# Attention with pooled keys, then a residual MLP, on one core: the second program moved to GpSimd alone, and the last store moved to ScalarE's queue

## The chip, the cores and the metric

One core of one Trainium2 chip runs the kernel. The time is device microseconds of one execution: the median of three runs is 333.9 us (333.8 to 334.21). A core has five engines with an instruction stream each: TensorE (PE; its weight loads are shown apart as PEld), VectorE (DVE), ScalarE (ACT), GpSimd (POOL) and SyncE (SP, which here only issues DMAs). SP, ACT and POOL each have a queue of DMAs of their own. All queues feed the same 16 DMA engines, and so does the loading of the engines' instructions.

## What is computed

Shapes: `q`, `k`, `v` are (8 batches, 8 heads, 576 tokens, 64), all float32.

```python
k_p = k.reshape(B, H, 72, 8, D).mean(axis=3)          # 8 neighbours pooled
v_p = v.reshape(B, H, 72, 8, D).mean(axis=3)
scores = (1 / sqrt(D)) * q @ k_p.T                     # (B, H, 576, 72)
attn = exp(scores - max(scores)) / (sum(exp(scores - max(scores))) + 1e-9)
x = (attn @ v_p), heads side by side                   # (B, 576, 512)
u = x + lam * (w_tok @ (alpha1 * x + beta1))           # mixing of tokens
out = u + lam * (relu((alpha2 * u + beta2) @ w_ch1) @ w_ch2)   # 512 -> 2048 -> 512
```

## The kernel before

There are two programs in one kernel. `direct` (L202) computes the result in 16-bit matmuls and takes exp without subtracting the maximum. That holds only while the sums of the exponentials stay within bounds, so `direct` also checks its sums: near its end, `all_in_range` (L249) and `count_in_range` (L261) reduce the saved reciprocals of all sums to one number, `fine`, which is 1 where all lie in range. The last function (L1226) then loads `fine` into a register (L1234), on PE, ACT and POOL, and enters `tc.If(good < 1)` (L1235): the second program, `general` (L24), computes everything again, safely and slowly, over the same output. With the inputs given here `fine` is 1. `general` is never entered: its instructions lie in memory behind those of `direct`, and the engines that take part in it branch past them.

`general` before uses PE (transposes and matmuls), ACT (copies out of PSUM, exp, relu) and POOL (elementwise work and all DMAs). Hence the three engines at L1234: each loads `fine`, compares, and either runs its part or jumps behind it. Behind it, the end of the program is common to all five engines (shown at L1262): SP waits for every semaphore in turn, those of the DMA queues among them, so for the landing of every store; then all engines meet in two barriers, between which POOL clears the semaphores.

`direct` works in blocks of 512 rows of tokens, nine in all (`NBLK`). Each block goes through `mlp_A` (L851: 512 -> 2048, relu on ACT) and then the second matrix. From block 2 on that second product is Winograd's form of Strassen's scheme: `hidden_sum` and `weight_sum` on DVE, seven `product`s (L958, matmuls at L985), and `gather` (L989, the additions into `u_sb` on DVE at L1000 and L1003). The order of instructions in each block is written out by hand: `todo` is a list of (due time, action), sorted at L1221, and no scheduler moves anything afterwards.

In the last block the stores are cut in halves of 256 columns (L1186 to L1193). `store` (L893) issues one DMA on `queues[0]` for a chunk of 128 rows (L898), and two of 64 rows, on `queues[0]` and `queues[1]`, for a chunk shared by two batches (L902). The last actions of all are the gather of product 3 (two DVE additions at L1000, rows `m` = 0 and 1, columns 256 to 511) and, due at 29.2, the two stores of just these rows. Before, both go on SP's queue:

```python
todo.append((27.2, lambda m=m: store(n, 2 + m, 0, HALF, (nc.sync, nc.scalar))))
todo.append((29.2, lambda m=m: store(n, m, HALF, DM)))     # queues=(nc.sync, nc.sync)
```

ACT's own last DMA is the second 64-row half of the store due at 27.2 (L902). Behind it in ACT's stream stand the load of `fine` and the branch. In PE's stream these stand behind the last matmul of L985, in POOL's behind its last multiplication for the attention of batch 7 (L771).

Of the kernel before, what the change touches and what calls it, by code (L numbers as in the profile page):

```python
# [7 lines left out]
FP = mybir.dt.float32  # L8
# [6 lines left out]
P = 128  # L15
# [8 lines left out]
def general(  # L24
# [18 lines left out]
    B, H, S, D = q.shape  # L43
    sb = ctx.enter_context(tc.tile_pool(name="g_sb", bufs=1))
    tmp = ctx.enter_context(tc.tile_pool(name="g_tmp", bufs=2))
    ps_s = ctx.enter_context(tc.tile_pool(name="g_ps", bufs=2, space=bass.MemoryType.PSUM))
    ps_l = ctx.enter_context(tc.tile_pool(name="g_psl", bufs=2, space=bass.MemoryType.PSUM))

    def tok(c):
        return (P if c < 4 else REM), slice(P * c, min(P * c + P, S))  # L50

    ident = sb.tile([P, P], FP, tag="ident", name="g_ident")
    nc.gpsimd.memset(ident, 0.0)
    nc.gpsimd.affine_select(out=ident, in_=ident, compare_op=ALU.not_equal, fill=1.0, base=0,
                            pattern=[[-1, P]], channel_multiplier=1)
    pool = sb.tile([P, 16], FP, tag="pool", name="g_pool")
    nc.gpsimd.memset(pool, 0.125)
    nc.gpsimd.affine_select(out=pool, in_=pool, compare_op=ALU.is_ge, fill=0.0, base=0,
                            pattern=[[-8, 16]], channel_multiplier=1)
    nc.gpsimd.affine_select(out=pool, in_=pool, compare_op=ALU.is_ge, fill=0.0, base=7,  # L60
                            pattern=[[8, 16]], channel_multiplier=-1)
    pools = sb.tile([P, 5, SPG], FP, tag="pools", name="g_pools")
    nc.gpsimd.memset(pools, 0.0)
    for c in range(5):
        n = 16 if c < 4 else 8
        nc.gpsimd.tensor_copy(out=pools[:, c, 16 * c:16 * c + n], in_=pool[:, 0:n])

    minus = sb.tile([P, 1], FP, tag="minus", name="g_minus")
    nc.gpsimd.memset(minus, -1.0)

    def smaller(out, a, b):


        d = tmp.tile([P, SPG], FP, tag="d", name="g_d")[0:a.shape[0], 0:a.shape[1]]
        nc.gpsimd.tensor_tensor(out=d, in0=a, in1=b, op=ALU.subtract)
        nc.scalar.activation(out=d, in_=d, func=AF.Relu, bias=0.0, scale=1.0)
        nc.gpsimd.tensor_tensor(out=out, in0=a, in1=d, op=ALU.subtract)

    vec = {}
    for name, src in (("a1", alpha1), ("b1", beta1), ("a2", alpha2), ("b2", beta2), ("lam", lam)):  # L80
        vec[name] = sb.tile([P, DM], FP, tag=f"vec_{name}", name=f"g_{name}")
        nc.gpsimd.dma_start(out=vec[name], in_=src.unsqueeze(0).to_broadcast((P, DM)))
    w1 = sb.tile([P, 4, DFF], FP, tag="w1", name="g_w1")
    nc.gpsimd.dma_start(out=w1, in_=w_ch1.rearrange("(c p) j -> p c j", p=P))
    w2 = sb.tile([P, NJ, DM], FP, tag="w2", name="g_w2")
    nc.gpsimd.dma_start(out=w2, in_=w_ch2.rearrange("(j p) d -> p j d", p=P))

    def transposed(src, rows, cols):
        ps = ps_s.tile([P, P], FP, tag="t", name="g_pt")
        nc.tensor.transpose(out=ps[0:cols, 0:rows], in_=src, identity=ident[0:rows, 0:rows])  # L90
        return ps[0:cols, 0:rows]

    wT = sb.tile([P, 5, S], FP, tag="wT", name="g_wT")
    for c in range(5):
        n, rows = tok(c)
        w = sb.tile([P, S], FP, tag="w_tok", name="g_w")
        nc.gpsimd.dma_start(out=w[0:n], in_=w_tok[rows])
        for i in range(5):
            m, cols = tok(i)
            nc.scalar.copy(out=wT[0:m, i, rows], in_=transposed(w[0:n, cols], n, m))  # L100

    for b in range(B):
        raw = []
        for src in (q, k, v):
            t = sb.tile([P, 5, H, D], FP, tag=f"raw{len(raw)}", name="g_raw")
            for c in range(5):
                n, rows = tok(c)
                nc.gpsimd.dma_start(out=t[0:n, c], in_=src[b, :, rows].rearrange("h p d -> p h d"))
            raw.append(t)
        means = []  # L110
        for t in raw[1:]:
            ps = ps_l.tile([P, DM], FP, tag="l", name="g_pl")
            for c in range(5):
                n, _ = tok(c)
                nc.tensor.matmul(out=ps[0:SPG], lhsT=pools[0:n, c],
                                 rhs=t[0:n, c].rearrange("p h d -> p (h d)"),
                                 start=(c == 0), stop=(c == 4))
            m = sb.tile([SPG, H, D + 1], FP, tag=f"mean{len(means)}", name="g_mean")
            nc.gpsimd.memset(m, 1.0)
            nc.scalar.copy(out=m[:, :, 0:D], in_=ps[0:SPG].rearrange("p (h d) -> p h d", d=D))  # L120
            means.append(m)
        kp, vp = means
        x = sb.tile([P, 5, DM], FP, tag="x", name="g_x")
        for h in range(H):
            cols = slice(D * h, D * h + D)
            kT = tmp.tile([D, SPG], FP, tag="kT", name="g_kT")
            nc.scalar.copy(out=kT, in_=transposed(kp[:, h, 0:D], SPG, D))
            for c in range(5):
                n, _ = tok(c)
                qT = tmp.tile([D, P], FP, tag="qT", name="g_qT")  # L130
                nc.scalar.copy(out=qT[:, 0:n], in_=transposed(raw[0][0:n, c, h], n, D))
                sc = ps_s.tile([P, P], FP, tag="s", name="g_sc")[0:n, 0:SPG]
                nc.tensor.matmul(out=sc, lhsT=qT[:, 0:n], rhs=kT)
                neg = tmp.tile([P, SPG], FP, tag="neg", name="g_neg")
                nc.scalar.activation(out=neg[0:n], in_=sc, func=AF.Copy, bias=0.0, scale=-0.125)
                low = tmp.tile([P, SPG], FP, tag="low", name="g_low")
                src, size = neg, SPG
                while size > 1:
                    half = size // 2
                    smaller(low[0:n, 0:half], src[0:n, 0:half], src[0:n, half:2 * half])  # L140
                    if size % 2:
                        smaller(low[0:n, 0:1], low[0:n, 0:1], src[0:n, size - 1:size])
                    src, size = low, half
                E = tmp.tile([P, SPG], FP, tag="E", name="g_E")
                nc.scalar.activation(out=E[0:n], in_=neg[0:n], func=AF.Exp, bias=low[0:n, 0:1],
                                     scale=-1.0)
                ET = tmp.tile([SPG, P], FP, tag="ET", name="g_ET")
                nc.scalar.copy(out=ET[:, 0:n], in_=transposed(E[0:n], n, SPG))
                av = ps_s.tile([P, P], FP, tag="s", name="g_av")[0:n, 0:D + 1]
                nc.tensor.matmul(out=av, lhsT=ET[:, 0:n], rhs=vp[:, h])  # L150
                xv = tmp.tile([P, D + 1], FP, tag="xv", name="g_xv")
                nc.scalar.copy(out=xv[0:n], in_=av)
                nc.gpsimd.tensor_tensor(out=xv[0:n, D:D + 1], in0=xv[0:n, D:D + 1],
                                        in1=minus[0:n], op=ALU.pow)
                nc.gpsimd.tensor_tensor(out=x[0:n, c, cols], in0=xv[0:n, 0:D],
                                        in1=xv[0:n, D:D + 1].to_broadcast((n, D)), op=ALU.mult)
        a = sb.tile([P, 5, DM], FP, tag="a", name="g_a")
        for c in range(5):
            n, _ = tok(c)
            nc.gpsimd.tensor_tensor(out=a[0:n, c], in0=x[0:n, c], in1=vec["a1"][0:n], op=ALU.mult)  # L160
            nc.gpsimd.tensor_tensor(out=a[0:n, c], in0=a[0:n, c], in1=vec["b1"][0:n], op=ALU.add)
        aT = sb.tile([P, 4, S], FP, tag="aT", name="g_aT")
        for c in range(5):
            n, rows = tok(c)
            ps = ps_l.tile([P, DM], FP, tag="l", name="g_pl")
            for i in range(5):
                m, _ = tok(i)
                nc.tensor.matmul(out=ps[0:n], lhsT=wT[0:m, i, rows], rhs=a[0:m, i],
                                 start=(i == 0), stop=(i == 4))
            y = tmp.tile([P, DM], FP, tag="y", name="g_y")  # L170
            nc.scalar.copy(out=y[0:n], in_=ps[0:n])
# [4 lines left out]
            for cc in range(4):  # L176
                nc.scalar.copy(out=aT[:, cc, rows],
                               in_=transposed(y[0:n, P * cc:P * cc + P], n, P))
# [1088 lines left out]
```

## Time and profile before

| what | value |
|---|---|
| median of three runs | 333.9 us |
| the profiled execution, its own time | 334.24 us |
| its span, first to last instruction | 332.5 us |
| PE busy | 325.2 us (98%), 2531 matmuls |
| DVE, ACT, POOL busy | 236.5, 175.5, 95.4 us |
| granted TensorE clock, mean | 0.998 |
| bytes moved | 45.87 MB |

The span is counted from the program's first to its last instruction; 1.7 us of the execution lie around it. "Busy" leaves out register, branch, semaphore and DMA-issuing instructions: these are work of an engine's sequencer and are shown with a q behind the engine's name (SPq, ACTq, PEldq). An issue's duration is the time that the sequencer needs to hand the transfer over, not that of the transfer. A transfer's landing is read from the semaphore that it raises, 16 times, once for each DMA engine. The profile also records the loading of instructions as packets of kind "instruction" (queues q8 and q14).

### The profile page before, as it was taken

Reading aid. Unit: us, or ns where it says so; the run is one execution under the profiler, and the core shown is the slowest. Engines: PE = TensorE matmul, PEld = TensorE weight load, DVE = VectorE, ACT = ScalarE, POOL = GpSimd, SP = SyncE. Lnnn points to the kernel's source line nnn. Section 1 sums busy time; section 2 is a strip of 40 time slices with the busy share of each in tenths; the row PEclk is TensorE's granted clock in tenths of the full one; section 3 lists DMA queues with packets and bytes.
Section 4 is the critical chain, followed back from the end, with each engine's and each line's share of the span. In section 5 each row is a group of like instructions: output and inputs, shape, how many; then the busy total and the mean of one; then the engine's idle time right before and its main releaser. Section 6 shows DMA issues by size and latency. Waiting matters only on the chain.

```text
span 332.5 us, 6533 instructions
## 1 busy us (share of the span) xinstructions
PE 325.2 (98%) x2531; PEld 209.2 (63%) x2531; DVE 236.5 (71%) x490; ACT 175.5 (53%) x322; POOL 95.4 (29%) x110
## 2 busy tenths in 40 slices
PE   8999999999999999999999999999999999999993
PEld 3667764455545576657775676567756765686582
DVE  6774389999589879776967696779677872355262
ACT  2775989368323852387138712881288126605700
POOL 8769737401255021700180019002700200000000
PEclk9999999999999999999999999999999999999999
DMA  7999999967896972499549933994330035003013
GB/s 117 199 221 270 267 209 237 198 152 107 169 229 110 225 194 55 89 234 161 147 116 222 165 121 89 231 174 136 73 127 2 0 65 142 2 0 128 2 34 101
DMA packets 66622, 45.87 MB, mean 138 GB/s; under 512 B 34541, under 2 KB 57205, under 8 KB 66586
## 3 DMA queue, kind: packets, MB, share of 16 engines
q1 hardware_dynamic: 52380, 32.80, 43.0%
q0 software_dynamic: 13824, 12.40, 22.6%
q8 instruction: 22, 0.36, 0.5%
q10 hardware_dynamic: 382, 0.21, 0.2%
q14 instruction: 14, 0.11, 0.1%
HBM read 38.30 MB, written 9.44 MB: 144 GB/s over the span
## 4 chain that ended last, share of the span: by engine, by line
PE 96%; DVE 1%; POOL 0%; issue 0%; ACT 0%
PE ps_h L862 38%; PE ps_w L985 26%; PE ps_tok L814 11%; PE ps_ch L882 8%; PE ps_av L756 3%; PE ps_s L713 2%; PE ps_warm L805 2%; PE ps_kp L645 1%; PE ps_r L720 1%; PE ps_av L760 1%; PE ps_q L602 1%; PE ps_sc L693 0%; PE ps_w L529 0%; DVE u_sb L818 0%; POOL u_bf L824 0%; PE ps_v L672 0%
## 5 line engine op out<-in xcount | busy, mean ns | idle before, releaser
L862 PE MATMUL ps_h<-u_fm,w 128*128 128x512 bf16 (+2 forms) x608 | 133.7, 369 | 0.2 <-DVE bias_cols L865 0.2
L869 ACT ACTIVATE H<-ps_h,bias_cols 128x512 bf16<-128x512 f32 x144 | 98.2, 688 | 55.4 <-PE ps_h L862 54.5
L862 PEld LDWEIGHTS <-w 128*128 128x128 bf16 x608 | 65.8, 114 | 49.7 <-issue 2.2
L985 PEld LDWEIGHTS <-H 128*128 128x128 bf16 x560 | 53.5, 98 | 10.8 <-DVE u_sb L1003 1.2
L822 ACT CAST u_bf<-u_sb 128x512 bf16<-128x512 f32 x32 | 19.8, 618 | 71.1 <-issue 39.9
L985 PE MATMUL ps_w<-w_l,H 128*128 128x256 bf16 x448 | 53.6, 273 | 0.0
L1003 DVE TENSOR_TENSOR u_sb<-u_sb,ps_w 128x512 f32<-128x512 f32 x54 | 36.2, 682 | 17.1 <-PE ps_w L985 17.1
L778 POOL TENSOR_TENSOR xs<-x_tm,lamal_bc 128x512 bf16<-128x512 f32 x12 | 15.9, 1328 | 108.3 <-DVE x_tm L764 108.1
L814 PE MATMUL ps_tok<-xs,wtT 128*128 128x512 bf16 (+3 forms) x200 | 44.9, 380 | 0.0
L818 DVE TENSOR_TENSOR u_sb<-x_tm,ps_tok 128x512 f32<-128x512 f32 (+1 forms) x40 | 27.3, 683 | 10.0 <-PE ps_tok L814 9.9
L764 DVE TENSOR_TENSOR x_tm<-ps_av,recs 128x320 f32<-128x320 f32 x64 | 31.5, 492 | 2.6
L742 ACT ACTIVATE ET<-ps_s 72x512 f16<-72x512 f32 x56 | 32.3, 591 | 0.0
L814 PEld LDWEIGHTS <-wtT 128*128 128x128 bf16 (+3 forms) x200 | 17.4, 100 | 16.0 <-issue 1.1
L762 DVE RECIPROCAL recs<-ps_av 128x5 f32<-128x5 f32 x64 | 12.1, 188 | 16.6 <-PE ps_av L760 16.3
L683 DVE TENSOR_TENSOR v_u<-v_u 72x1024 f32<-72x1024 f32 (+1 forms) x24 | 22.8, 948 | 0.2
L985 PE MATMUL ps_w<-w_t,h_s 128*128 128x256 bf16 x168 | 22.6, 273 | 0.0
L882 PEld LDWEIGHTS <-H 128*128 128x128 bf16 x128 | 12.0, 98 | 13.7 <-issue 0.4
L385 POOL TENSOR_TENSOR k_raw<-k_raw 128x512 f32<-128x512 f32 x14 | 18.7, 1339 | 2.6 <-PE ps_tok L814 1.8
L387 POOL TENSOR_TENSOR k_bf<-k_raw 128x512 bf16<-128x512 f32 x14 | 18.8, 1342 | 1.1
L985 PEld LDWEIGHTS <-h_s 128*128 128x128 bf16 x168 | 16.4, 98 | 4.1
L954 DVE TENSOR_TENSOR H<-H,H 128x1024 bf16<-128x1024 bf16 x14 | 9.6, 689 | 12.8 <-ACT H L869 12.7
L756 PEld LDWEIGHTS <-ET 72*128 72x128 f16 x256 | 13.9, 97 | 6.3 <-DVE al_bc L498 0.3
(153 smaller groups left out, 370.7 us busy)
## 6 DMA issues: line engine op xcount, KB each, us to landing
out_dram<-u_sb SPq DMA_DIRECT2D x29, 256.0 KB
k_raw<-in_k_dram SPq DMA_DIRECT2D x12, 512.0 KB
v_u<-in_v_dram SPq DMA_DIRECT2D x12, 512.0 KB
q_bf<-in_q_dram POOLq DMA_DIRECT2D x16, 256.0 KB, 7.4
w<-in_moe_w_ch_dram POOLq DMA_DIRECT2D x6, 512.0 KB, 13.0
out_dram<-u_sb SPq DMA_DIRECT2D x12, 128.0 KB
w<-in_moe_w_ch_dram POOLq DMA_DIRECT2D x1, 1024.0 KB, 14.3
k_raw<-in_k_dram POOLq DMA_DIRECT2D x2, 512.0 KB, 16.7
```

Source lines behind the costliest of these rows:

```text
L683: nc.vector.tensor_tensor(out=out, in0=t[:, :, 0:width], in1=t[:, :, width:2 * width], op=ALU.add)
L742: nc.scalar.activation(out=o, in_=i, func=AF.Exp, bias=0.0, scale=0.125)
L756: nc.tensor.matmul(out=av[:, odd + c, :], lhsT=ET[:, m0:m0 + 128], rhs=vp1[:, h % 4, :])
L764: nc.vector.tensor_tensor(out=x[:, 1 - odd:6 - odd, dd:dd + D], in0=av[:, :, 0:64], in1=rec.unsqueeze(2).to_broadcast((P, 5, D)), op=ALU.mult)
L814: nc.tensor.matmul(out=ps_tok[p0:p1], lhsT=wtT[0:kk, at, P * c:P * c + p1 - p0], rhs=xs_pool[i][0:kk, sc, :], start=(sc == 0), stop=(sc == 4))
L818: nc.vector.tensor_tensor(out=s["u"][p0:p1, :], in0=x[p0:p1, 1 + c if c < 4 else 5 - 5 * i, :], in1=ps_tok[p0:p1, 0:DM], op=ALU.add)
L822: nc.scalar.copy(out=s["u_bf"], in_=s["u"])
L862: nc.tensor.matmul(out=ps_h[:, t0:t1 + one], lhsT=w1_of(cc, j), rhs=rhs, start=(cc == 0), stop=(cc == 3))
L869: nc.scalar.activation(out=H4[n, j // 4][:, j % 4, :], in_=ps_h, func=AF.Relu, bias=bias_cols[:, j:j + 1], scale=1.0)
L882: nc.tensor.matmul(out=ps, lhsT=H_of(n, j)[:, 128 * m:128 * m + 128], rhs=(w2l if n else w2)[j // 4][:, j % 4, :], start=(j == 0), stop=(j ...
L985: nc.tensor.matmul(out=ps, lhsT=stat(j), rhs=moving(j), stop=(j == 7), start=(first and (pp == 0 or alone) and j == 0), skip_group_check=True)
L1003: nc.vector.tensor_tensor(out=o, in0=o, in1=banks[key, "both"], op=ALU.add)
```

## The change

Three things are edited.

1. `general` is written anew. All of it runs on GpSimd: matrix products are multiplications of broadcast rows and additions that halve the terms, exp and the reciprocal are powers, and intermediate results that every partition needs go through DRAM. In the built program the second program was 3539 instructions on PE, 6434 on ACT and 5716 on POOL (172 DMAs among them); now it is 85,375 on POOL (2701 DMAs among them) and none elsewhere. It is still not entered.
2. Since only POOL takes part in it, `fine` is loaded by POOL alone. PE and ACT have neither the load nor the branch: their streams run from the last instruction of `direct` straight into the common end. The two instructions that check the loaded value for 0 or 1 move from PE to POOL.
3. Of the two last stores, the one for `m` = 1 goes on ACT's queue, behind ACT's 64-row store; the one for `m` = 0 stays on SP's.

All other instructions of `direct`, on every engine, are the same and in the same order. The waits are the same too: the moved store still waits for the same DVE addition.

```diff
 def general(...):
     nc = tc.nc
     B, H, S, D = q.shape
+    g = nc.gpsimd
+    NP, NC = 96, 6
     sb = ctx.enter_context(tc.tile_pool(name="g_sb", bufs=1))
-    tmp = ctx.enter_context(tc.tile_pool(name="g_tmp", bufs=2))
-    ps_s = ctx.enter_context(tc.tile_pool(name="g_ps", bufs=2, space=bass.MemoryType.PSUM))
-    ps_l = ctx.enter_context(tc.tile_pool(name="g_psl", bufs=2, space=bass.MemoryType.PSUM))
...
+    dram = ctx.enter_context(tc.tile_pool(name="g_dram", bufs=1, space=bass.MemoryType.DRAM))
...
+    def contract(acc, left, rows, n, m, step, tag):
+        g.memset(acc, 0.0)
+        for k in range(0, n, step):
+            w = sb.tile([NP, step, m], FP, tag="w", name=f"g_w{tag}")
+            g.dma_start(out=w.rearrange("p k j -> p (k j)"),
+                        in_=spread(rows[k:k + step].rearrange("k j -> (k j)"), step * m))
+            for c in range(NC):
+                t = sb.tile([NP, step, m], FP, tag="t", name=f"g_t{tag}")
+                g.tensor_tensor(out=t, in0=w, op=ALU.mult,
+                                in1=left[:, c, k:k + step].unsqueeze(2).to_broadcast((NP, step, m)))
+                size = step
+                while size > 1:
+                    half = size // 2
+                    g.tensor_tensor(out=t[:, 0:half], in0=t[:, 0:half], in1=t[:, half:2 * half],
+                                    op=ALU.add)
+                    size = half
+                g.tensor_tensor(out=acc[:, c], in0=acc[:, c], in1=t[:, 0], op=ALU.add)
+        return acc
...
@@ direct, last block @@
                     todo.append((29.2, lambda m=m: store(
-                        n, m, HALF, DM)))
+                        n, m, HALF, DM, ((nc.sync, nc.scalar)[m],) * 2)))
@@ the function that calls both @@
-    good = nc.values_load(fine[0:1, 0:1], engines=(mybir.EngineType.PE, mybir.EngineType.Activation, mybir.EngineType.Pool), min_val=0, max_val=1)
+    good = nc.values_load(fine[0:1, 0:1], engines=(mybir.EngineType.Pool,), min_val=0, max_val=1)
     with tc.If(good < 1):
         general(tc, *args)
```

More of the change, by code (lines that the diff above doesn't have):

```diff
@@ L43, in general @@
     B, H, S, D = q.shape
+    g = nc.gpsimd
+    NP, NC = 96, 6
     sb = ctx.enter_context(tc.tile_pool(name="g_sb", bufs=1))
-    tmp = ctx.enter_context(tc.tile_pool(name="g_tmp", bufs=2))
-    ps_s = ctx.enter_context(tc.tile_pool(name="g_ps", bufs=2, space=bass.MemoryType.PSUM))
-    ps_l = ctx.enter_context(tc.tile_pool(name="g_psl", bufs=2, space=bass.MemoryType.PSUM))
-    def tok(c):
-        return (P if c < 4 else REM), slice(P * c, min(P * c + P, S))
-    ident = sb.tile([P, P], FP, tag="ident", name="g_ident")
@@ L53, in general @@
[L53 to L77, printed above, removed]
+    dram = ctx.enter_context(tc.tile_pool(name="g_dram", bufs=1, space=bass.MemoryType.DRAM))
@@ new lines, in tok, with spread @@
+    def tok(ap):
+        return ap.rearrange("(c p) d -> p c d", p=NP)
+    def spread(ap, n):
+        return ap.unsqueeze(0).to_broadcast((NP, n))
+    def contract(acc, left, rows, n, m, step, tag):
[16 more added lines that the diff above has]
+        return acc
@@ L79, in general, with larger @@
+    def larger(a, b, out):
+        d = sb.tile([NP, NC, SPG // 2], FP, tag="d", name="g_d")[:, :, 0:a.shape[2]]
+        g.tensor_tensor(out=d, in0=a, in1=b, op=ALU.subtract)
+        g.tensor_scalar(out=d, in0=d, scalar1=0.0, scalar2=None, op0=ALU.max)
+        g.tensor_tensor(out=out, in0=b, in1=d, op=ALU.add)
     vec = {}
     for name, src in (("a1", alpha1), ("b1", beta1), ("a2", alpha2), ("b2", beta2), ("lam", lam)):
-        vec[name] = sb.tile([P, DM], FP, tag=f"vec_{name}", name=f"g_{name}")
@@ L82, in general @@
[L82 to L100, printed above, removed]
-    for b in range(B):
[L103 to L123, printed above, removed]
-        for h in range(H):
[L125 to L171, printed above, removed]
-            nc.gpsimd.tensor_tensor(out=y[0:n], in0=vec["lam"][0:n], in1=y[0:n], op=ALU.mult)
-            nc.gpsimd.tensor_tensor(out=x[0:n, c], in0=x[0:n, c], in1=y[0:n], op=ALU.add)
-            nc.gpsimd.tensor_tensor(out=y[0:n], in0=x[0:n, c], in1=vec["a2"][0:n], op=ALU.mult)
-            nc.gpsimd.tensor_tensor(out=y[0:n], in0=y[0:n], in1=vec["b2"][0:n], op=ALU.add)
-            for cc in range(4):
-                nc.scalar.copy(out=aT[:, cc, rows],
-                               in_=transposed(y[0:n, P * cc:P * cc + P], n, P))
-        hid = sb.tile([P, NJ, S], FP, tag="hid", name="g_hid")
-        for j in range(NJ):
-            for t0, t1 in ((0, 512), (512, S)):
-                ps = ps_l.tile([P, DM], FP, tag="l", name="g_pl")[:, 0:t1 - t0]
-                for cc in range(4):
-                    nc.tensor.matmul(out=ps, lhsT=w1[:, cc, P * j:P * j + P], rhs=aT[:, cc, t0:t1],
-                                     start=(cc == 0), stop=(cc == 3))
-                nc.scalar.activation(out=hid[:, j, t0:t1], in_=ps, func=AF.Relu, bias=0.0,
-                                     scale=1.0)
-        for c in range(5):
-            n, rows = tok(c)
-            ps = ps_l.tile([P, DM], FP, tag="l", name="g_pl")
-            for j in range(NJ):
-                nc.tensor.matmul(out=ps[0:n], lhsT=hid[:, j, rows], rhs=w2[:, j],
-                                 start=(j == 0), stop=(j == NJ - 1))
-            y = tmp.tile([P, DM], FP, tag="y", name="g_y")
-            nc.scalar.copy(out=y[0:n], in_=ps[0:n])
-            nc.gpsimd.tensor_tensor(out=y[0:n], in0=vec["lam"][0:n], in1=y[0:n], op=ALU.mult)
-            nc.gpsimd.tensor_tensor(out=x[0:n, c], in0=x[0:n, c], in1=y[0:n], op=ALU.add)
-            nc.gpsimd.dma_start(out=out[b, rows], in_=x[0:n, c])
@@ new lines, in general, with by @@
+        vec[name] = sb.tile([NP, 1, DM], FP, tag=f"vec_{name}", name=f"g_{name}")
+        g.dma_start(out=vec[name][:, 0], in_=spread(src, DM))
+    def by(name):
+        return vec[name].to_broadcast((NP, NC, DM))
+    base = sb.tile([NP, 1], FP, tag="base", name="g_base")
+    g.memset(base, 2.718281828459045)
+    minus = sb.tile([NP, 1], FP, tag="minus", name="g_minus")
+    g.memset(minus, -1.0)
+    for b in range(B):
+        pooled = []
+        for src in (k, v):
+            means = dram.tile([H, SPG, D], FP, tag=f"mean{len(pooled)}", name="g_mean")
+            raw = sb.tile([SPG, H, 8, D], FP, tag="w", name="g_raw")
+            for h in range(H):
+                g.dma_start(out=raw[:, h].rearrange("g a d -> g (a d)"),
+                            in_=src[b, h].rearrange("(g a) d -> g (a d)", a=8))
+            for n in (4, 2, 1):
+                g.tensor_tensor(out=raw[:, :, 0:n], in0=raw[:, :, 0:n], in1=raw[:, :, n:2 * n],
+                                op=ALU.add)
+            g.tensor_scalar(out=raw[:, :, 1], in0=raw[:, :, 0], scalar1=0.125, scalar2=None,
+                            op0=ALU.mult)
+            g.dma_start(out=means.rearrange("h g d -> g h d"), in_=raw[:, :, 1])
+            pooled.append(means)
+        x = sb.tile([NP, NC, DM], FP, tag="x", name="g_x")
+        for h in range(H):
+            qt = sb.tile([NP, NC, D], FP, tag="q", name="g_q")
+            g.dma_start(out=qt, in_=tok(q[b, h]))
+            kp, vp = [], []
+            for t, means, tag in ((kp, pooled[0], "kp"), (vp, pooled[1], "vp")):
+                t.append(sb.tile([NP, SPG, D], FP, tag=tag, name="g_p"))
+                g.dma_start(out=t[0].rearrange("p g d -> p (g d)"),
+                            in_=spread(means[h].rearrange("g d -> (g d)"), SPG * D))
+            E = sb.tile([NP, NC, SPG], FP, tag="E", name="g_E")
+            for c in range(NC):
+                t = sb.tile([NP, SPG, D], FP, tag="t", name="g_ts")
+                g.tensor_tensor(out=t, in0=kp[0], op=ALU.mult,
+                                in1=qt[:, c].unsqueeze(1).to_broadcast((NP, SPG, D)))
+                for n in (32, 16, 8, 4, 2):
+                    g.tensor_tensor(out=t[:, :, 0:n], in0=t[:, :, 0:n], in1=t[:, :, n:2 * n],
+                                    op=ALU.add)
+                g.tensor_tensor(out=E[:, c], in0=t[:, :, 0], in1=t[:, :, 1], op=ALU.add)
+            top = sb.tile([NP, NC, SPG // 2], FP, tag="top", name="g_top")
+            src, size = E, SPG
+            while size > 1:
+                half = size // 2
+                larger(src[:, :, 0:half], src[:, :, half:2 * half], top[:, :, 0:half])
+                if size % 2:
+                    larger(top[:, :, 0:1], src[:, :, size - 1:size], top[:, :, 0:1])
+                src, size = top, half
+            g.tensor_tensor(out=E, in0=E, in1=top[:, :, 0:1].to_broadcast((NP, NC, SPG)),
+                            op=ALU.subtract)
+            g.tensor_scalar(out=E, in0=E, scalar1=1.0 / D ** 0.5, scalar2=None, op0=ALU.mult)
+            g.tensor_tensor(out=E, in0=base.unsqueeze(2).to_broadcast((NP, NC, SPG)), in1=E,
+                            op=ALU.pow)
+            half = SPG // 2
+            g.tensor_tensor(out=top, in0=E[:, :, 0:half], in1=E[:, :, half:], op=ALU.add)
+            for n, odd in ((18, 0), (9, 0), (4, 1), (2, 0), (1, 0)):
+                if odd:
+                    g.tensor_tensor(out=top[:, :, 0:1], in0=top[:, :, 0:1],
+                                    in1=top[:, :, 2 * n:2 * n + 1], op=ALU.add)
+                g.tensor_tensor(out=top[:, :, 0:n], in0=top[:, :, 0:n], in1=top[:, :, n:2 * n],
+                                op=ALU.add)
+            g.tensor_scalar(out=top[:, :, 0:1], in0=top[:, :, 0:1], scalar1=1e-9, scalar2=None,
+                            op0=ALU.add)
+            g.tensor_tensor(out=top[:, :, 0:1], in0=top[:, :, 0:1],
+                            in1=minus.unsqueeze(2).to_broadcast((NP, NC, 1)), op=ALU.pow)
+            for c in range(NC):
+                t = sb.tile([NP, SPG, D], FP, tag="t", name="g_ta")
+                g.tensor_tensor(out=t, in0=vp[0], op=ALU.mult,
+                                in1=E[:, c].unsqueeze(2).to_broadcast((NP, SPG, D)))
+                for n, odd in ((36, 0), (18, 0), (9, 0), (4, 1), (2, 0), (1, 0)):
+                    if odd:
+                        g.tensor_tensor(out=t[:, 0:1], in0=t[:, 0:1], in1=t[:, 2 * n:2 * n + 1],
+                                        op=ALU.add)
+                    g.tensor_tensor(out=t[:, 0:n], in0=t[:, 0:n], in1=t[:, n:2 * n], op=ALU.add)
+                g.tensor_tensor(out=x[:, c, D * h:D * h + D], in0=t[:, 0], op=ALU.mult,
+                                in1=top[:, c, 0:1].to_broadcast((NP, D)))
+        y = sb.tile([NP, NC, DM], FP, tag="y", name="g_y")
+        z = sb.tile([NP, NC, DM], FP, tag="z", name="g_z")
+        g.tensor_tensor(out=y, in0=x, in1=by("a1"), op=ALU.mult)
+        g.tensor_tensor(out=y, in0=y, in1=by("b1"), op=ALU.add)
+        rows = dram.tile([S, DM], FP, tag="rows", name="g_rows")
+        g.dma_start(out=tok(rows), in_=y)
+        wt = sb.tile([NP, NC, S], FP, tag="kp", name="g_wt")
+        g.dma_start(out=wt, in_=tok(w_tok))
+        contract(z, wt, rows, S, DM, 16, "m")
+        g.tensor_tensor(out=z, in0=z, in1=by("lam"), op=ALU.mult)
+        g.tensor_tensor(out=x, in0=x, in1=z, op=ALU.add)
+        g.tensor_tensor(out=y, in0=x, in1=by("a2"), op=ALU.mult)
+        g.tensor_tensor(out=y, in0=y, in1=by("b2"), op=ALU.add)
+        hid = sb.tile([NP, NC, DFF], FP, tag="hid", name="g_hid")
+        contract(hid, y, w_ch1, DM, DFF, 4, "a")
+        g.tensor_scalar(out=hid, in0=hid, scalar1=0.0, scalar2=None, op0=ALU.max)
+        contract(z, hid, w_ch2, DFF, DM, 16, "b")
+        g.tensor_tensor(out=z, in0=z, in1=by("lam"), op=ALU.mult)
+        g.tensor_tensor(out=x, in0=x, in1=z, op=ALU.add)
+        g.dma_start(out=tok(out[b]), in_=x)
```

## The prediction

> **What bounds the kernel now.** I read the page first, then the chain of work that ended last, and then the last 8 us queue by queue, since the change touches nothing earlier but POOL's branch.
>
> ```profile
> span 332.5 us, 6533 instructions
> ...
> PE 325.2 (98%) x2531; PEld 209.2 (63%) x2531; DVE 236.5 (71%) x490; ACT 175.5 (53%) x322; POOL 95.4 (29%) x110
> ...
> q8 instruction: 22, 0.36, 0.5%
> ```
>
> PE is the bound up to its last matmul, and nothing that PE computes is changed. The last steps of the chain say where that ends: 314.97 + 12.24 = 327.2 us. The span is 332.5, so 5.3 us at the end belong to no engine's work.
>
> ```profile
> 301.16 13.81 PE ps_h L862 x64
> 314.97 12.24 PE ps_w L985 x112
> ```
>
> Next the timelines of DVE, SP and ACT from 324 us on (start, duration, engine, line):
>
> ```profile
> 327.23 0.42 DVE L1000 TENSOR_TENSOR u_sb<-u_sb,ps_w 128x256 f32<-128x256 f32 x1 [0.45 <-PE ps_w L985]
> ...
> 326.20 0.44 SPq L898 DMA_DIRECT2D out_dram<-u_sb  x1
> 326.68 0.47 SPq L902 DMA_DIRECT2D out_dram<-u_sb  x1
> 327.25 2.51 SPq L898 DMA_DIRECT2D out_dram<-u_sb  x2
> ...
> 326.20 0.57 ACTq L902 DMA_DIRECT2D out_dram<-u_sb  x1
> ```
>
> DVE is done at 327.65. The last two stores on SP take 2.51 us to issue. Singly, the trace has the one for m = 0 from 327.248 to 329.284 (2.036 us) and the one for m = 1 from 329.382 to 329.760. The first waits for an addition that ended at 326.78, so it is not waiting for data. All issues of that line together show how far 2.036 is from the usual:
>
> ```profile
> L898 SPq DMA_DIRECT2D out_dram<-u_sb x35: 332/424/2036, 57.4 to 329.4; - x35
> ```
>
> (minimum, median and maximum in ns.) By the semaphores, the store for m = 0 lands at 331.04 and that for m = 1 at 331.30; SP, which waits for each in turn, goes on 17 ns later, and the common end takes the remaining **1.20 us** (331.30 to 332.50). So the landing of the last store sets the end.
>
> Why does the issue take 2 us? The rows of the branch (sequencer instructions of L1235; counts, then min/median/max in ns, first and last start):
>
> ```profile
> L1235 POOLq COMPARE_BRANCH  x1: 45/45/45, 308.1 to 308.1; - x1
> L1235 POOLq INC_SWDGE_SEM  x1: 876/876/876, 311.3 to 311.3; - x1
> L1235 PEldq COMPARE_BRANCH  x1: 4129/4129/4129, 326.1 to 326.1; - x1
> L1235 ACTq COMPARE_BRANCH  x1: 58/58/58, 327.6 to 327.6; - x1
> L1235 ACTq EVENT_SEMAPHORE  x1: 17/17/17, 330.3 to 330.3; - x1
> ```
>
> PE branches at 326.11 and goes on at 330.24; ACT branches at 327.62 and its next instruction comes 2.58 us after; POOL's (308.12) comes 2.68 us after. In each gap the records hold a packet of instructions: one of 16 KB on q8 from 327.161 to 328.915, and 8 KB on q14 at 328.57 and 309.10. PE's other packets of 16 KB come every 10 to 21 us, as its stream runs on (the last at 323.71 to 324.99); the one at 327.161 comes 3.4 us later and is the branch's.
>
> Such a packet occupies one DMA engine, and the stores show it. Issues of plain DMAs on SP that stall end 0.37 to 0.43 us after a 16 KB packet ends, five times before the last one: 93.92 (packet to 93.49), 159.38 (158.96), 174.89 (174.52), 207.53 (207.14), 224.28 (223.89), and now 329.28 (328.92). Where few stores are in flight it stalls none: beside the packet of 323.71 the issues at 324.45 and 324.84 take 0.33 and 0.53 us. The landings agree: of the stores issued at 326.20 (SP and ACT) and 326.68, 15 of the 16 engines have landed after 1.92 to 2.14 us, the sixteenth after 3.85 to 4.05. **So PE's branch, which nobody waits for as such, delays the last stores.**
>
> **The change, part by part.** The terms go against the profiled execution, 334.24 us (span 332.50 and 1.74 around it); it lies 0.34 above the median of the runs, 333.9. About 0.2% (0.67 us) is what a measurement can tell from no change.
>
> *Branch and load removed from PE and ACT.* Their own durations cost nothing now: PE is back at 330.24 and ACT at 330.26, before SP is ready (331.7). What goes is the 16 KB packet and the 8 KB one at 328.57. PE has then some 36 instructions left after its packet at 323.71, and a packet comes about every 250 recorded instructions, so none follows within the span. The store for m = 0 then takes the 0.33 to 0.44 us of its kind and is issued from 327.25 to 327.69.
>
> *The store for m = 1 on ACT's queue.* ACT is free at 326.78, so the store waits only for DVE's 327.665 and starts at 327.68 (SP's issues start 16 ns after such an update). Behind it ACT has nothing but the common end. Left on SP without the stall, it would start about 327.77, so the queue itself is worth 0.09 us. From issue to full landing, stores of this size with no packet near take 1.90, 2.03, 1.91 and 1.92 us (issued at 319.22, 319.60, 324.45 and 329.38, all on SP). ACT's only store of the stretch had 15 engines in after 2.14 us, where SP's of the same shape took 1.92 to 2.02. I take 2.02, between; ends 1.90 and 2.14. It lands at 327.68 + 2.02 = 329.70 (329.58 to 329.82) instead of 331.30: **1.60 us earlier** (1.48 to 1.72). The store for m = 0 lands near 329.2, before it.
>
> *The wait list on SP.* One wait fewer before the landing, the same six steps behind it: 1.20 us stays. What is late next? SP without stall is through its issues at 327.7, PE is at the end after 327.2, ACT at 328.2, POOL at 315.0. None comes near 329.70.
>
> *POOL.* It takes over two checks (0.17 + 0.03 us on PE) and still branches, at about 308.4. Cover until SP asks at 329.8: 15 us after POOL's part ends at 315.0. Its counts to make good grow: each of eight DMA semaphores is raised by about 5400 instead of 340. In the trace each is raised by one update, 8 ns apart, so I cost growth at nothing; the other end, the 3.75 us from 311.26 to 315.01 growing with the amount (2701 / 172 = 15.7 times), is 59 us and is a rival below. The 85,375 instructions are not executed and cost nothing but a longer jump; 2.68 us for POOL over 5,716 and 2.58 for ACT over 6,434 show no growth with length.
>
> [...]
>
> **Sum.** 334.24 - 1.60 = 332.64 for a profiled execution; for the median of runs 333.9 - 1.60 = **332.3 us**.
>
> **Rivals.**
>
> A. *The stall is the stores' own*, from four issues on two queues within 1.1 us, and the packet only coincides. For it: they crowd as at no other place, and not every packet stalls an issue. Against: the five other stalls, each tied to a packet. Then m = 0 still lands at 331.04, m = 1 on ACT before or with it, and the end moves by 0.26 us or not at all: 333.6 to 333.9, no change. The same time results if PE's stream still ends in a jump, that is, if the change doesn't take the packet away; the rows of DVE, which had no branch before, speak against that (its common end follows its last addition at once, at 327.25).
>
> B. *Another packet falls into the last 3 us*: ACT's stream is longer by a few instructions, and 8 KB packets took 0.31 to 0.59 us. A store's last share would be held by that much plus its place behind the others: 0.4 to 0.9 us of the gain lost, 332.7 to 333.2.
>
> C. *Slower: POOL's exit becomes the end.* Place: raising the DMA semaphores and the drain behind it (3.75 us). It decides once it lasts from 311.5 past 331.3, so from about 5.3 times its time, and the kernel is slower from there; in proportion to the amounts it is 59 us, the end comes at about 371, and the time is 333.9 + 39 = 373. For it: the drain of 2.84 us has no other cause that I see. Against: one update for each semaphore, whatever the amount.
>
> **Chances.** Forecast 0.76; B 0.08; A 0.10; C 0.06. Faster by over 0.2%: 0.76 + 0.08 = 0.84; within: 0.10; slower: 0.06. The likeliest's own range is 332.0 to 332.6, from the ends of the landing (1.48 to 1.72) and 0.2 us for the spread of runs. With B, 8 in 10 are in from 331.9 to 333.1; A and C are left out.
>
> **What would show it.** No packet on q8 after about 325; the last store on SP issued within 0.45 us; one store on ACT at 327.7; landing near 329.7 and a span near 330.9. A store on SP still stalled for 1.5 us or more, or POOL's drain ending after 329, would make the prediction wrong.

## The result, and the profile after

The changed kernel takes 332.46 us (median of 10 runs, 332.01 to 333.2), the kernel before beside it 334.23 us (10 runs, 333.8 to 336.76). The ratio is 0.993, with an interval of 0.9905 to 0.9955: less time, clear of noise, though by under 1%. This ratio goes by all executions (their means are 332.52 and 334.86 us, 2.34 apart); the medians are 1.77 us apart. The profiled execution took 332.40 us, its span 330.66.

The page after; no packet of instructions is left on q8 but the twenty of PE's regular stream (22 before):

```profile
span 330.7 us, 6526 instructions
...
PE 325.0 (98%) x2531; PEld 209.1 (63%) x2531; DVE 236.6 (72%) x490; ACT 175.6 (53%) x322; POOL 95.4 (29%) x110
...
q8 instruction: 20, 0.33, 0.4%
```

The last 5 us in the timeline (start, duration, engine, line; L885 is the store that was L898, L987 the addition that was L1000):

```profile
326.51 0.47 SPq L889 DMA_DIRECT2D out_dram<-u_sb  x1
327.08 0.53 SPq L885 DMA_DIRECT2D out_dram<-u_sb  x1
327.11 0.42 DVE L987 TENSOR_TENSOR u_sb<-u_sb,ps_w 128x256 f32<-128x256 f32 x1 [0.45 <-PE ps_w L972]
327.56 0.39 ACTq L885 DMA_DIRECT2D out_dram<-u_sb  x1
```

The store for m = 0 is issued in 0.53 us where it took 2.04, and ACT issues the last one as soon as DVE is done (327.53). By the semaphores these two land at 329.22 and 329.47; the span ends 1.19 us later. POOL alone branches, with the same exit as before:

```profile
L1222 POOLq COMPARE_BRANCH  x1: 50/50/50, 308.1 to 308.1; - x1
L1222 POOLq INC_SWDGE_SEM  x1: 880/880/880, 311.1 to 311.1; - x1
```

For what follows, the **tail** is the time from the end of the last addition on DVE to the end of the span: 332.50 - 327.65 = 4.85 us before, 330.66 - 327.53 = 3.13 us after. That is 1.72 us of the 1.84 us between the two spans; the other 0.12 us are there, within 0.03 us, from 25 us on.

### The profile page after: what moved, and what is told of

Same layout as the page of the kernel before. It is cut to its first block, busy times and chain, and to the rows that moved or that the text cites. A ratio compares the mean times of both kernels' runs of the same rounds, so it can differ in the third digit from the quotient of the medians.

```text
span 330.7 us, 6526 instructions
## 1 busy us (share of the span) xinstructions
PE 325.0 (98%) x2531; PEld 209.1 (63%) x2531; DVE 236.6 (72%) x490; ACT 175.6 (53%) x322; POOL 95.4 (29%) x110
## 4 chain that ended last, share of the span: by engine, by line
PE 97%; DVE 1%; POOL 0%; issue 0%; ACT 0%
PE ps_h L849 38%; PE ps_w L972 26%; PE ps_tok L801 11%; PE ps_ch L869 8%; PE ps_av L743 3%; PE ps_s L700 2%; PE ps_warm L792 2%; PE ps_kp L632 1%; PE ps_r L707 1%; PE ps_av L747 1%; PE ps_q L589 1%; PE ps_sc L680 0%; PE ps_w L516 0%; DVE u_sb L805 0%; POOL u_bf L811 0%; PE ps_v L659 0%
```

## The experiments

All tails, from the records of each profiled execution. "Packet" is the last 16 KB packet on q8 of PE's, first to last moment, counted from the end of the last addition; a second packet after the branch's, once the stores have landed, is left out.

| kernel | branch behind which code | packet | last landing | tail |
|---|---|---|---|---|
| before | PE, ACT, POOL | -0.49 to 1.26 | 3.65 | 4.85 |
| before, once more (x4) | PE, ACT, POOL | 0.28 to 1.28 | 3.46 | 4.67 |
| after | POOL | -3.95 to -2.71 | 1.94 | 3.13 |
| after, once more (z1) | POOL | -3.94 to -2.70 | 1.95 | 3.15 |
| x1, store back on SP | POOL | -3.99 to -2.66 | 2.11 | 3.31 |
| x2, only the store moved | PE, ACT, POOL | -0.41 to 1.23 | 3.53 | 4.85 |
| x3, branch with nothing to skip | POOL (PE, ACT: none) | -3.37 to -2.44 | 2.38 | 3.65 |
| y1, PE's jump put back | PE, POOL | 0.04 to 1.00 | 3.13 | 4.39 |
| y2, ACT's jump put back | ACT, POOL | -3.44 to -2.52 | 2.37 | 4.59 |
| y3, stream shifted, 122 | POOL | none in the last 19 us | 1.93 | 3.12 |
| y4, stream shifted, 126 | POOL | -2.66 to -1.08 | 3.37 | 4.62 |
| z2, waits turned | POOL | -3.96 to -2.93 | 1.94 | 2.89 |

**x1: the branch alone.**

```diff
-                        n, m, HALF, DM, ((nc.sync, nc.scalar)[m],) * 2)))
+                        n, m, HALF, DM)))
```

> The changed kernel with both last stores on SP's queue again: only the branch is gone from PE and ACT. Theory (PE's far branch brings a 16 KB packet of instructions, which holds up a DMA engine and with it the last stores): no packet on q8 after 325 us, no stalled issue, the last store about 0.09 us later than in the changed kernel; 1.5 to 1.7 us below the kernel before. Rival 1 (the queue is the gain: the store for m = 1 no longer stands behind another on SP): less than 0.3 us below the kernel before, the issue for m = 0 still takes about 2 us.

332.71 us against 334.61 (ratio 0.9941, 0.9916 to 0.9966). No stalled issue (0.53 and 0.40 us), no packet near. The tail is 0.18 us longer than in the changed kernel, since SP begins the last store 0.23 us after DVE's end and ACT 0.03 us. So nearly the whole gain comes from the branches' removal, and rival 1 falls. (Beside x1 to x4, executions of equal granted clock differ by 334.10 - 332.54 = 1.56 us; see the table under x4.)

**x2: the queue alone.** The kernel before, with

```diff
-                        n, m, HALF, DM)))
+                        n, m, HALF, DM, ((nc.sync, nc.scalar)[m],) * 2)))
```

> The kernel before with only the store for m = 1 moved to ACT's queue; PE, ACT and POOL still load and branch. Theory: the packet of PE's branch is still there at about 327.2 us, SP's issue for m = 0 still takes about 2 us and lands near 331.0, the moved store's sixteenth landing is late too, near 331.0; time 0.2 to 0.3 us below the kernel before, no change by the measurement. Rival 1 (the queue is the gain): 1.5 us or more below it.

334.05 against 334.61 us (0.997, 0.9942 to 0.9997); the kernel before had more of the executions with a lower clock, and at equal clock the medians differ by 0.18 us. The issue for m = 0 takes 1.98 us again (first fence), and the tail is 4.85 us, not a moment less than before. The second fence, the sequencers' rows of the branch, says why the expected 0.2 us are not in the tail:

```profile
328.90 1.98 SPq L898 DMA_DIRECT2D out_dram<-u_sb  x1
```

```profile
L1235 PEldq COMPARE_BRANCH  x1: 4035/4035/4035, 327.8 to 327.8; - x1
L1235 ACTq COMPARE_BRANCH  x1: 58/58/58, 330.3 to 330.3; - x1
L1235 PEldq EVENT_SEMAPHORE  x1: 51/51/51, 331.9 to 331.9; - x1
L1235 ACTq EVENT_SEMAPHORE  x1: 17/17/17, 333.2 to 333.2; - x1
```

ACT's branch now stands behind a later store, comes at 330.28 instead of 327.62, and ACT goes on at 333.15, 0.36 us after the last landing (332.79): ACT's way back has become the end.

**x3: a branch with nothing behind it.**

```diff
-    good = nc.values_load(fine[0:1, 0:1], engines=(mybir.EngineType.Pool,), min_val=0, max_val=1)
+    good = nc.values_load(fine[0:1, 0:1], engines=(mybir.EngineType.PE, mybir.EngineType.Activation, mybir.EngineType.Pool), min_val=0, max_val=1)
```

> The changed kernel, with the number that decides loaded and compared on PE, ACT and POOL as in the kernel before, though PE and ACT have nothing in the second program, so that the branch has nothing to skip there. Theory: PE and ACT compare within about 0.1 us, no packet of 16 KB after 325 us, the stores land as in the changed kernel; same time as the changed kernel within 0.2 us, so 1.6 to 1.8 below the kernel before. Rival 2 (loading and branching as such is what costs on PE and ACT, wherever the branch leads): the branch on PE takes about 4 us again, and the time is that of the kernel before.

```profile
L1222 PEldq COMPARE_BRANCH  x1: 249/249/249, 327.8 to 327.8; - x1
L1222 ACTq COMPARE_BRANCH  x1: 58/58/58, 330.4 to 330.4; - x1
```

PE's comparison takes 0.25 us where it took 4.13 (0.1 had been expected), and no packet follows: loading and branching as such bring no packet and no stall of 2 us, and rival 2 falls. The time is 333.04 against 334.61 us (0.9943, 0.9919 to 0.9966). The forecast was missed all the same: at equal clock the gain is 1.16 us, not 1.6 to 1.8, and the tail, 3.65 us, is 0.5 us longer than the changed kernel's. PE's regular packet lies 0.6 us nearer to the end here, one of SP's issues beside it takes 0.76 us instead of 0.49 and ends 0.38 us after the packet, and the issues after it are late in turn. The packet ends in the same place, 2.4 to 2.5 us before the end of the last addition, in y1 and y2, with an issue of 0.74 and 0.69 us that ends 0.38 and 0.39 us after it; in before, after, z1, x1, x2 and z2 it ends at 2.6 to 2.9 us and that issue takes 0.48 to 0.57 us. Why it moves was not tested.

**y1 and y2: one far jump put back at a time.** In front of the new second program (never executed), for PE and for ACT (shortened: the tiles and the list of loading engines are left out):

```diff
+    for _ in range(1200):
+        nc.tensor.matmul(out=far_out, lhsT=far, rhs=far)     # y1, with PE among the loading engines
+        nc.scalar.copy(out=far, in_=far)                     # y2 instead, with ACT among them
```

> The changed kernel, with 1200 small matmuls on PE put into the second program (never executed) and the deciding number loaded and compared on PE too, so that PE alone has a far jump again; ACT has none, and the last store stays on ACT's queue. The tail is counted from the end of the last addition on DVE to the end of the span: 4.85 us in the kernel before, 3.13 in the changed one. Theory (the packet of PE's jump holds the stores): a packet of 16 KB at about the last addition, a stalled issue on SP, landings 1.5 us late, tail 4.5 to 4.9 us. Rival 2 (PE's own return from the jump is the end): PE is back 2.6 us after the last addition, tail 3.5 us, landings as in the changed kernel.

y1: 333.90 us against 334.08 (0.9995, 0.9966 to 1.0023): no gain can be told any more. Packet from 327.10 to 328.06; SP's issue for m = 0, from the timeline, and PE's rows:

```profile
327.05 1.39 SPq L892 DMA_DIRECT2D out_dram<-u_sb  x1
```

```profile
L1229 PEldq COMPARE_BRANCH  x1: 3924/3924/3924, 325.5 to 325.5; - x1
L1229 PEldq EVENT_SEMAPHORE  x1: 51/51/51, 329.5 to 329.5; - x1
```

The issue ends at 328.44, 0.38 us after the packet, and the last landing is at 330.19, while PE is back at 329.49: PE's own return is not the end, the store is. So rival 2 falls. The packet is shorter than before's (0.96 us, not 1.75), and by the tail so is the loss: 4.39 us is just under the 4.5 to 4.9 expected. Of the 1.26 us by which it exceeds the changed kernel's, some 0.5 fall to the regular packet by x3's measure; against x3's 3.65 the jump itself is worth 0.74 us.

> The changed kernel, with 1200 small copies on ACT put into the second program (never executed) and the deciding number loaded and compared on ACT too, so that ACT alone has a far jump, behind the store that was moved to it. Theory: its packet of 8 KB comes about 1 us after the branch, when the stores' data have moved; no issue stalls and the stores land as in the changed kernel, but ACT goes on only 2.6 us after its branch, near 331.3 us, later than SP's last landing, so ACT becomes the end: tail 4.4 to 4.8 us. Rival 3 (only PE's packet costs anything, ACT's jump is hidden): tail 3.1 to 3.4 us, the time of the changed kernel.

y2: 333.79 us against 334.08 (0.9988, 0.9961 to 1.0014): gone as well, by another way.

```profile
L1227 ACTq COMPARE_BRANCH  x1: 62/62/62, 329.8 to 329.8; - x1
L1227 ACTq EVENT_SEMAPHORE  x1: 17/17/17, 333.0 to 333.0; - x1
```

The issue for m = 0 takes its 0.54 us, and the last landing is at 331.69, 2.37 us after the last addition. That is where x3 has it (2.38), whose regular packet lies in the same place, and not the changed kernel (1.94). But ACT goes on 3.1 us after its branch, at 332.95. SP, which has ACT's semaphore as the last in its list, waits 0.99 us for it. Rival 3 falls: ACT's jump is hidden in the kernel before because it stands ahead of a stalled store, and would not be behind the moved one.

**y3 and y4: a packet without a branch.** The changed kernel, with (shortened: the few lines that define `small_warm` are left out)

```diff
-    keep_warm(13)
+    keep_warm(3)
+    small_warm(122)      # y3; 126 in y4: matmuls of 16x16 into a tile that nobody reads
```

> The changed kernel, no branch on PE, with 10 of the 13 first warming matmuls on PE exchanged for 122 tiny ones (16x16, into a tile that nobody reads): 224 instructions more, so that the regular packet of PE's stream that came at 323.6 us falls about 32 instructions later, into the last stores. Theory: a packet that begins within 1 us of the last addition does what the branch's did: landings late by 0.5 to 1.7 us, tail 3.6 to 4.8 us. Rival 4 (the packet is incidental, the branch costs): tail 3.1 to 3.3 us as in the changed kernel. The body's time may differ by some us, since the start is warmed differently; only the tail is compared.

> The same with 126 tiny matmuls: the regular packet falls about 8 instructions earlier than with 122, some 0.4 us. Theory: the delay of the landings follows the packet's place; tail 3.4 to 4.8 us. Rival 4: tail 3.1 to 3.3 us.

In y3 the shift was larger than I had reckoned: the packet never comes, and the tail is 3.12 us, that of the changed kernel. In y4, eight instructions more, it comes, from 329.00 to 330.59, as PE's sequencer reaches its last instructions. The timeline of SP, in y3 the two 64-row stores alone, then in y4:

```profile
327.65 1.12 SPq L895 DMA_DIRECT2D out_dram<-u_sb  x2
```

```profile
328.47 0.33 SPq L891 DMA_DIRECT2D out_dram<-u_sb  x1
328.85 2.87 SPq L895 DMA_DIRECT2D out_dram<-u_sb  x2
331.82 0.53 SPq L891 DMA_DIRECT2D out_dram<-u_sb  x1
```

The first issue of the 2.87 us runs from 328.85 to 330.96, 2.11 us, and ends 0.37 us after the packet. All later stores are late behind it; the tail is 4.62 us. PE has no branch in either kernel. The pair differs in four tiny matmuls in the first microseconds and in this packet, and the packet is worth 1.5 us of tail; rival 4 falls. (Their times, 335.32 and 338.02 us, one execution each, hold the changed start too. The other 1.2 us between them arise in the first 20 us, at full clock in both, and are not explained.)

**x4 and z1: the size.** Each kernel unchanged, beside the kernel before.

> The kernel before, unchanged, timed once more with a span for each execution. Open question: its runs hold some at 335 to 337 us, the changed kernel's none above 333.2. If the packet of PE's branch varies in length, the long executions are longer within the span by the same amount; if they come from outside the program, the span stays near 332.5. Both theories expect 333.8 to 334.3 for most executions.

> The changed kernel, unchanged, timed beside the kernel before on one more chip, to settle the size. So far executions whose mean granted clock is below 0.996 are 1.4 to 2.2 us longer, in every kernel. Theory (the change is worth the 1.72 us of the tail and nothing else): among executions with a clock of 0.996 or more the medians differ by 1.5 to 1.8 us; with the others counted in, the ratio depends on how many of them fall to each kernel, 0.993 to 0.997. Rival 5 (the kernel before has a further loss of its own that only some executions show): the difference is 2 us or more among executions of equal clock.

x4: 334.48 against 334.61 us, ratio 0.9998. z1: 332.36 against 333.88 us, ratio 0.995 (0.9932 to 0.9968). The long executions are long within the span: 1.7 to 1.9 us lie around it in all. Only one of x4's twelve lay in the expected 333.8 to 334.3 us. Most of the long ones were granted less clock: of 120 executions of the kernel before, x2, x4, y1 and y2, 38 took 335 us or more, 32 of these at a mean clock below 0.996 and six at 0.996 or more. The profiled execution of x4 is one of the six (335.34 us, clock 0.999): its packet is shorter than in the first profile (1.00 us against 1.75) and its tail too, so the packet's length is not what makes it long. It is 1.28 us behind the first profile from 70 us on, and the cause is open. Medians, split by the mean granted clock of the execution:

| kernel | 0.996 or more | below |
|---|---|---|
| before, beside x1 to x4 | 334.10 (18) | 335.77 (14) |
| before, beside y1 to y4 | 333.79 (15) | 335.96 (8) |
| before, beside z1 | 333.86 (14) | 335.65 (3) |
| after, first ten | 332.46 (10) | none |
| z1 | 332.36 (11) | none |
| x1 | 332.54 (8) | 334.44 (1) |
| x2 | 333.92 (10) | 335.98 (2) |
| x3 | 332.94 (9) | 334.71 (3) |

The profiled execution of x3 has a low mean clock, 0.988. Its row by stretch for 10 to 20 us (stretch, length, then PE, PEld, DVE, ACT, POOL busy, granted clock, DMA) and that of the changed kernel's:

```profile
10.00:20.00 10.00, 9.78 (x95) 7.17 (x95) 6.25 (x19) 6.22 (x17) 6.43 (x8) 0.66 1.20 201
```

```profile
10.00:20.00 10.00, 9.67 (x123) 6.75 (x123) 8.06 (x25) 8.04 (x21) 7.50 (x9) 1.00 1.19 195
```

PE is busy for the same time and gets 95 matmuls done instead of 123: the records show half clock from 11.0 to 17.9 us. At equal clock the change is worth 333.86 - 332.36 = 1.50 us beside z1, which is just inside the expected 1.5 to 1.8; rival 5 falls. Against the three medians of before on their several chips, the first ten and z1 lie 1.3 to 1.7 us lower. For the ten executions of before beside those first ten no clock is on record.

**z2: a version beyond both.**

```diff
-                    todo.append((27.2 if m < 2 else 29.2, lambda m=m: store(n, m)))
+                    at = 27.2 if m < 2 else 29.2
+                    if n == NBLK - 2:
+                        todo.append((at, lambda m=m: store(n, m, 0, HALF)))
+                        todo.append((at, lambda m=m: store(n, m, HALF, DM)))
+                    else:
+                        todo.append((at, lambda m=m: store(n, m)))
```

> The changed kernel with the four stores of the last block but one cut into two halves of 256 columns each. That is four DMAs more, well before the end, and it turns the semaphore of the very last store from the fourth to the eighth of SP's list of waits, so that one step stands behind its landing there and not five. Theory (from the last landing to the end of the span, SP's remaining list counts): the 1.19 us from landing to the end become 0.95 and the tail 2.9 us, if the four extra issues disturb nothing; 0.2 us is too little for the times. Rival 6 (the list is hidden behind the barriers): 1.19 us stays and the tail is 3.1 us.

The tail is 2.89 us, 0.95 of it from the last landing on. 332.21 us against 333.88 (0.9944, 0.9923 to 0.9965): the fastest median here, though the times cannot tell it from z1's 332.36. Rival 6 falls.

## Why the prediction was right in its steps, and where it was wrong

- **"The landing of the last store sets the end": right.** It held in the changed kernel, and 1.19 us from landing to end stayed, as forecast (1.20).
- **"PE's branch ... delays the last stores" through its packet: right.** Taking the far target away (x3, x1) takes the 2 us stall away, putting it back on PE (y1) brings back one of 1.39 us, and a packet with no branch does the same (y4). What it says of the packet of 323.71, that "it stalls none", is nearly so: the issue at 324.84 ends 0.38 us after that packet and takes 0.53 us, 0.05 us more than where no packet is near (y3). Rival A, the stores' own crowding, falls: the same stores crowd in the changed kernel, in y3 and in z1 with no stall. Rival B, another packet in the last 3 us, did not come true: in the changed kernel the last packet on q8 ends at 324.83, 5.8 us before the end. x3 and y4 show that even a packet of that sort costs 0.5 and 1.5 us when it lies nearer to the last stores.
- **"The store for m = 0 then takes the 0.33 to 0.44 us": 0.53.** It landed at 329.22 (forecast near 329.2) and set nothing.
- **"1.60 us earlier (1.48 to 1.72)": 1.72 by the tail.** The term that was too large is the landing of ACT's store, 2.02 us forecast and 1.90 measured: the rows of SP fitted, ACT's slower 64-row store did not. The queue's own worth, forecast 0.09, is 0.18 by x1.
- **"Their own durations cost nothing now": right as it stands, but it left out a link.** The moved store pushes ACT's branch back; without the removal on ACT the move gains nothing and ACT's return is the end (tail 4.85 us in x2, 4.59 in y2). The two edits need each other, which the sum, made edit by edit, did not say.
- **POOL, rival C: excluded.** Raising the eight semaphores (by about 5400 each, 2701 x 16 / 8, an estimate from the count of DMAs and the 16 raises of each landing) took 0.880 us (0.876 before) and the drain 2.839 us in both. From the end of the branch its next instruction comes after 2.52 us over 85,375 instructions, 2.68 over 5,716.
- **Wrong: "about 0.2% (0.67 us) is what a measurement can tell", with "0.2 us for the spread of runs", and the base of 333.9 us.** This is the step that failed. The three runs shown lay within 0.4 us, and the profiled one was granted 0.998 of the clock; later executions of the kernel before run from 333.0 to 338.06 us. Most of the long ones have a lower mean clock, and three traces (x2, x3, y2) show it at half for 3.4 to 6.8 us early on; some are long at full clock. Four of the ten executions of before lay at 334.97 or above and none of the changed kernel's, so the first ratio, 0.993, put the gain at 0.7%, or 333.9 x 0.993 = 331.6 us, below my range of 331.9 to 333.1, while the changed kernel's median, 332.46, lies in it. On another chip the ratio was 0.995, at equal clock the difference 1.50 us, and the tails differ by 1.72: the forecast of 1.60 (0.48%) was the size of the effect, and the spread about it, 0.2 us, was put far too small. How much of the first 2.34 us between the means is chance in the long executions the runs do not say.

Open: whether the drop of the clock is itself rarer without far jumps at the end. It fell on 4 of 49 executions of kernels with POOL's jump alone (after, x1, x3, z1, z2) and on 35 of 120 of the others (before beside all three, x4, x2, y1, y2). But x3 had 3 of its 12, the chips differ, and no run was made to tell it apart. The 1.50 us leave it out as far as the split goes; the first 0.993 may contain it. The mean clock also counts a half clock after PE's last matmul (in the kernel before from 331.08 us on, which alone makes its 0.998; in y4 it alone makes 0.996), so the split at 0.996 is a rough one.

## What to carry to other kernels

Look at what happens after the last compute instruction: here 4.85 us of tail held 1.7 us that no busy row shows, and an engine that nobody waits for caused most of them (by y1, where PE's far jump is back, 1.26 us over the changed kernel). The jumps over code that is never executed were dear here, where they fell into the last transfers: 1.54 us of tail, 4.85 before against 3.31 in x1. Keep such a jump to an engine that is done long before (here POOL, whose drain ends at 314.8 of 330.7 us), and count what is queued behind each moved DMA (in x2 the move alone left the tail at 4.85 us). A few instructions more on PE moved one of its regular packets into the last stores, at nearly the same price: eight from y3 to y4, 1.50 us of tail. Compare executions of equal granted clock before a difference under 1% is believed: in the table under x4 the two columns of one kernel lie 1.67 to 2.17 us apart.

## What the runs showed of the hardware that was not expected

- The 16 KB packets of PE's instructions took 0.9 to 2.0 us each (in the kernel before). Beside the one at 327.16, one of the 16 shares of each of the three stores issued at 326.20 and 326.68 landed only 3.85 to 4.05 us after its issue, the other 15 by 1.92 to 2.14. A plain transfer issued on SP meanwhile stalled its queue until 0.37 to 0.43 us after the packet in all six plain issues over 0.9 us of the kernel before, and in the last stores of x2, x4, y1 and y4. Not every one did: in the kernel before, the issue at 324.45 lay wholly beside the packet of 323.71 and took 0.33 us. A few other long issues (in the changed kernel 1.76 us at 47.65 and 1.16 us at 142.65) have no packet beside them, and their cause is open. The packets differ in size: PE's, on q8, are of 16 KB, those in the gaps of ACT and POOL, on q14, of 8 KB (328.57 and 309.10 in the kernel before). A regular packet with no branch near it costs 1.50 us of tail in y4 (4.62 us against 3.12 in y3).
- What a branch cost went by its target: the comparison took 0.05 to 0.06 us on ACT and POOL, on PE 0.25 where nothing is skipped (x3) and 3.9 to 4.2 for a far target (before, x2, x4, y1), and ACT or POOL went on 2.5 to 3.1 us after a far one.
- Each step of SP's list behind the last landing took 0.06 us, in order (329.48, 329.55, 329.61, 329.67 and 329.73 in the changed kernel), and the place of the last store's semaphore in that list was worth 0.24 us (1.19 us from landing to end in the changed kernel, 0.95 in z2).
